# A new order of issue for the whole program of a fused attention and token-mixing kernel

## The chip, the cores and the metric

The kernel runs on one core of one Trainium2 chip. The metric is the device time of one execution in microseconds (us); the time before is 207.22 us, the median of three runs (206.42 to 207.49). The engines are called by their short names: PE (TensorE matmul; PEld is its weight load), DVE (VectorE), ACT (ScalarE), POOL (GpSimd) and SP (SyncE, which here only issues DMAs).

## The reference

Batch 8, heads 8, sequence 576, head dimension 64; 8 x 64 = 512 channels.

```python
kv  = einsum('bhsd,bhse->bhde', k, v)
out = einsum('bhsd,bhde->bhse', q, kv)
rms = sqrt(mean(out*out, -1) + 1e-6)
x   = (out / rms * g_norm)            # heads side by side: (B, 576, 512)
theta = x @ w_theta
zr, zi = x*cos(theta), x*sin(theta)
y   = einsum('ts,bsd->btd', w_tok_r, zr) + einsum('ts,bsd->btd', w_tok_i, zi)
u   = x + y
return u + maximum(u @ w_ch, 0)
```

## The kernel before

The kernel is written as a list of 1189 small tasks, and a separate text, `TURNS`, says in which order they are issued. A task has a name, one or two engines that may run it, a function, and the tasks that it depends on. `play` walks through `TURNS`: a number n issues task n on its first engine, `n*` issues it on its second, and `rN` or `aN` issues N idle matmuls into a PSUM buffer of the `raw` or the `acc` kind. Each engine executes its own tasks strictly in the order in which they were issued, and waits at each for what it needs. So `TURNS` sets the order of every queue: PE, DVE, ACT, the DMAs that SP issues, and POOL with its own DMAs. The numbers shown in time order by the profile are the result of these five queues and their waits.

The 576 rows of a batch are four tiles of 128 (j = 0 to 3) and a tail of 64 (j = 4, marked `e` in names). For each batch b the tasks are, by name:

- **load** k, v (SP; for batch 0 also ACT), their tails (`k0e`, `v0e`), q and the weights (POOL). k and v have two buffers each, so the load of batch b waits for `kv` of batch b - 2. `hold p` is a POOL copy that reads one element of v's tails of batch 0 (L232), so the token weights' loads behind it on POOL are asked for only when those have landed; `hold w` reads the theta weight and holds the load of v of batch 1.
- **kv** (L255, PE): k'v for the heads, in fp32. In batch 0 it comes in pieces: `kvm 0 h` (full tiles of head pair h) and `kvt 0 h` (tails), two pairs to an accumulator. `ko2`/`ko4` (L275 on ACT, L277 on DVE) copy it into the block-diagonal `kbd`, each task as two casts.
- **qt**, `qo`: transpose of q (PE) and the copy `qT` out of PSUM; from batch 3 on q is transposed by a DMA (`qd`, SP).
- **raw** (L312, L321, PE): q times kv. `sq` (L334, ACT) squares, `ss` (L343, DVE) sums, `rt` (L353, POOL) takes the power -1/2, `x` (L375, L384, DVE) multiplies. For batch 0 the root goes by `rs` (L362, ACT) and `rt` (L351, DVE). `raw` has two PSUM buffers from batch 1 on; an `x` frees one.
- **xt**, `xc`: transpose of x (PE) and scaled copy `xT` (L408 on ACT, L410 on DVE); from batch 4 on the transpose is a DMA (`xd`, SP) and `xo` the scaled copy of 1024 columns.
- **th** (L440, L443, PE): theta. `pt` (L456, ACT) rounds the turns to int32, `ar` (L463, DVE) takes the fraction, `ab` (L471 on ACT, L473 on DVE) its absolute value, `si` and `co` (L481, L488, ACT) sine and cosine, `z` (L511, L500, DVE) the products with x.
- **wt** 0 to 8, `wo`: transposes of the token weights and their copies, once, in batch 0.
- **y0**, **y1** (L534, PE): the token mix, for columns 0 to 255 (`y0`) and 256 to 575 (`y1`) of four channel blocks, each in three parts of three matmuls. Part 0 needs z 0 and 1, part 1 needs z 2, part 2 all five. `um` (L539, DVE) makes u.
- **v** (L440, L443; L590 for the two halves of the last batch's tile 1, PE): the channel mix. `ut`, `uo` (or the DMA `ud`) bring u back to rows, `fin` (L576, L596, DVE) makes the output tile, `st` (L613, L617, L604) stores it from SP or POOL.

PSUM is shared by tags: two buffers `tr` for transposes, two `raw`, four `acc` for kv, theta, y and v. A task that opens such a tile waits until an earlier holder's readers are through. All these rules stand in the code as `takes` and `readers`.

Of the kernel before, what the change touches and what calls it, by code (L numbers as in the profile page):

```python
# [29 lines left out]


TURNS = """
3 4 0 1 2 5 6 7 9 8 11 10 13 29 30 41 r1 49 35 14 15 16 17 18 19 22 23 20 21 24 26 207 28 27 42* 57
58* 31 32 36 37 38 33* 34 39* 40* 73 43 74* 50* 44 45 59 75 51 65 25 60 12 61 76 46 66 77 47 62 63
52 r9 48 64 67 53 68 84 82 85 99 54 78 83* 69 70 100 135 139 136 140 79 80 71 55 56 72 92 90 91* 93
86 87* 127 88 101 89* 94 106 120 81 103 102 128* 95 131 137 113 132* 96 138* 104 121 122 105 129 97
114 107 130* 98 108 115 109 143 133 124 123* 134 169 173 141 161 210 211 212 213 110 125 111 144 117
116* 118 142 126 112 119 174 162 216 217* 214 215 170 230 163 223 218 219 231* 165 175 232 171 164
354 203 205 204 206 220 172 176 388 233 221 234 389 166 145 157 167 153 237 224 374 146 154 222 168
225 238* 235 226 236 155 156 227 147 149 244 239 158 375 245 240 251 150 151 187 159 252 241 228 242  # L40
261 253 262 188* 152 148 160 229 381 189 263 243 246 254 382 194 367 255 268 190 368* 256* 177 178*
275 257 182 247 265 264* 266 269 248 249 361 362 363 364 276 270 277 278 267 258* 250 183 279 271*
282 184 259 272 273 283 192 365* 366* 369 383 284 185 260 289 197 199 370 358 209 208 359 360 509
356 357 355 191 529 518 512 513 514 515 371 372 384 193 290 198 274 291 385 195 280 285* 373 281 200
386 292* 293 286 516 294 179 376 387 324 312 404 390 325 377 517 196 540 505 506 507 508 287 180 405
378 316 317 313 402 391 295 288 419 395 314 318 326 392 379 393 380 403 420 396 315 319 327 394 304
397 300 398 399 412 421 400 413 414 519 305 520 401 521 522 408 406 407 320 306 307 296 530 410 531
416 415 422* 423 424 417 411 301 409* 532 533 297 321 302 303 523 308 309 322 323 310 524 525 311
418 534 298 426 427 343 433 548 434 299 428 526 541 542 543 440 441 442 443* 435 544 186 511 527 430
429* 652 653 654 655 658 669 645 646 647 181* 510 425 549* 431 444 656 437 657 344* 545 345 546 554  # L50
563 436 432 555* 346 547* 528 564 445 565 348 584 349 535 536 438 328 556 338 467 468 475 659 585
557 446 439 537 586 339 469 470 558 476 477 455 340 451 452 588 660 329 661 649 785 651 538 650 539
787 662 341 456 670 453 454 560 559* 567 587* 671 672 663 561 457 550 447 552 471 472 458 553 478
673 674 347 680 648 686 473 474 675 333 335 334 336 794 337 805 783 330 676 677 331 577 664 463 589
566* 551 578 568 562 448 449 450 579 464 465 459 665 570 666 678 667 580* 581 571 569 572 466 582
460 461 574 687 668 573* 575 462 679 788 789 790 791 350 681 499 501 351 583 500 682 792 793 502 590
576 688 784 683 684 201* 921 479 699 700 692 693 694 795 489 490 591 685 701 332 503* 342 202 816
781 690 796 797 798 703 611 612 592 494 607 613 614 608 593 594 609 491 806 689* 713 702* 696 807
695* 697 492 808 610 595 619 620 621 481 495 484 596 597 698 799 809 714 715 810 623 782 822 493 930
704 480 482 800 598 622 599 600 811 706 801 802 707 812 705 708 710 709* 691* 615 616 603 604 605  # L60
813 485* 606 803 804 496 617 618 601 486 716* 717 602 786 814 639 817 720 641 487 818 640 819 497
642 924 925 926 927 820 815 821 823 721 722 723 711 718 712 719 928 929* 835 836 483 626 624 625 498
488 824 633 630 634 837 931 828 631 724 932 725 726 747 627 748 755 838* 628 749 936 750 756 727 829
937 938 830 933 743 744 745 757 758 746 735 728 729 730 636 632* 952 917 352* 826 941 919 918 939
934 504* 644* 825 849 751 637 739 740 940 741 947 832 839 831* 833 850 834 759 752 753 851 935 948
949 731 942 736 732 733 950 638* 754 742 842 737 853 840 852* 943 827 843 734 944 777 856 775 854
776 857 920 635 629 1059 951 738 953 760 762 761 945 1053 1054 1055 1056 844 841 946 858 845* 954
846 859* 955 855 778 847 860 956 957 848 1057 861 1058 922 958 1070 862 769 772 763 1060 863 864 770
773 1061 1062 865 959* 866 879 880 881 766 1065 1066 764 882 867 868 964 971 1063 1064 1071 1067 923
771 774* 960 962 1068 767 965 966 869 887 883 884 888 972 973 1069 885 871 1072 1073 765 643 353 895  # L70
1081 768* 1074 779* 974 870 886 967* 975 968 963 976 977 889 890 1075 872 992 1076 875 873 876 961
1077 993 874 994 877 891 892 893 969 996 995* 997 1078 878 978 979 894 970 985 980 986 982 981* 911
1082 913 912* 987 988* 983 914 998 984 908 899 905 1015 1016 989 990 896 780 897 898 1087 900 901
1079 991 999 1000 1017 1001 906 1018 1080 902 1011 1012 1013 903 1002 1083 1088 909 1014 1084 1093
1094 1095 1100 1101 1007 1008 1009 1019 1023 1102 1027 1028 1029 1024 1089 1085 916 1031 904 1086
1096* 1090 1097 1104 907 1091 910 1030 1103* 1025 1003 1004 1005 1020 1021 1010 1026 1006 1107 1022
1105 1098 1092 1106 1099 1108 1114 1115 1109 1121 1110 1047 1034 1033 1049 1048 1050 1116 1038 1041
1111 1122 1123 1112 1113 1124* 1125 1118 1126 1117* 1119 1032 1039 1040 1042 1043* 1156 1035 1036
1144 1157 1148 1149 1145 1152 1153 1127 1120 1146 1150 1154 1158 1151 1147 1155 1159 1037 1044 1136
1132 1045 1180 1178 1137 1138 1139 1179 1181 1133 1128 1183 1185 1173 1140 1141 1134 1184 1186 1129  # L80
1130 1135 1182 1188 1187 1131 1142 1143 1175 1160 1162 1046* 1174* 1176 1161* 1177 915* 1165 1163
1164 1051* 1167 1170 1052* 1166 1168 1171 1169 1172
""".split()


# [845 lines left out]
```

## Time and profile before

| | before |
|---|---|
| median of three runs | 207.22 us (206.42 to 207.49) |
| profiled execution, its own time | 206.56 us |
| span of the profile | 204.6 us |
| PE busy | 188.3 us in 2078 matmuls |
| DVE busy | 172.5 us in 362 instructions |
| ACT busy | 137.6 us in 272 |
| POOL busy | 86.4 us in 92 |
| data moved | 43.14 MB, mean 211 GB/s |

The span runs from the first to the last instruction of the program; the 2 us between it and the execution's own time lie outside. In the profile, "L255" is line 255 of the kernel. A row of a timeline or of the chain that ended last gives the start and the length in us, the engine, the line and the tile names; the chain merges neighbours of one kind (x80 is eighty instructions). In a group row the numbers after the bar are busy time, mean ns of one, and the idle time before them with what ended it. In a window row the values after the stretch are its length and, for PE, PEld, DVE, ACT and POOL, busy time with the count of instructions, then the granted clock, the DMA share and GB/s. A PE that is busy is not a PE at its peak: matmuls overlap, and a wait shorter than a matmul's own length leaves no idle time.

### The profile page before, as it was taken

The page shows a single profiled execution, that of the slowest core. Times are in us where ns is not written, and L with a number is a line of the kernel's source. Part 1 is how long each engine was busy: PE and PEld are TensorE (multiplying, and loading weights), DVE is VectorE, ACT ScalarE, POOL GpSimd, SP SyncE. Part 2 cuts the span into 40 slices and gives each one's busy share as a digit, 9 for nine tenths or more (in the row PEclk, how much of TensorE's full clock was granted, in tenths as well). Part 3 has the DMA queues.
Part 4 walks back from the last instruction along what each step waited for, and adds up shares of the span by engine and source line. Part 5 has one row for each costly group of instructions (what it writes and reads, how often), then busy time and mean ns, then how long its engine had stood idle before and what let it go on. Part 6 is the DMA issues. An engine that isn't in the chain of part 4 may idle for free.

```text
span 204.6 us, 5267 instructions
## 1 busy us (share of the span) xinstructions
PE 188.3 (92%) x2078; PEld 132.8 (65%) x2078; DVE 172.5 (84%) x362; ACT 137.6 (67%) x272; POOL 86.4 (42%) x92
## 2 busy tenths in 40 slices
PE   0299899999999999999999999998989999999992
PEld 0275568885786777676776767665856746755671
DVE  6029896789999999999898999897989999689473
ACT  2006899748799587987896769576945983976101
POOL 8022061263965564874609382283629430101210
PEclk9999999999999999999999999999999999999999
DMA  6999999999999999999999999799988652853154
GB/s 196 271 197 193 294 268 193 275 354 236 254 187 193 277 264 260 310 221 137 199 226 248 237 221 180 170 283 305 287 187 194 150 103 70 189 129 135 35 154 154
DMA packets 74951, 43.14 MB, mean 211 GB/s; under 512 B 44576, under 2 KB 71008, under 8 KB 74928
## 3 DMA queue, kind: packets, MB, share of 16 engines
q1 hardware_dynamic: 58688, 32.12, 66.9%
q0 software_dynamic: 15040, 9.52, 29.9%
q10 hardware_dynamic: 1200, 1.18, 1.7%
q8 instruction: 16, 0.26, 0.5%
q14 instruction: 7, 0.06, 0.1%
HBM read 33.06 MB, written 9.44 MB: 208 GB/s over the span
## 4 chain that ended last, share of the span: by engine, by line
PE 67%; ACT 12%; DVE 8%; DMA 7%; issue 2%; POOL 1%; DVEq 0%; ACTq 0%; POOLq 0%
PE y L534 29%; PE th L440 11%; PE v L440 11%; DMA vt<-in_v_dram 5%; PE kv L255 3%; PE raw L312 3%; DMA uD<-wn 2%; DVE arg L463 2%; ACT kbd L275 2%; ACT sc L488 2%; PE wps L630 2%; ACT sc L481 1%; ACT arg L471 1%; ACT xT L408 1%; PE qps L270 1%
## 5 line engine op out<-in xcount | busy, mean ns | idle before, releaser
L353 POOL TENSOR_TENSOR rt<-ss,mhalf 128x8 f32<-128x8 f32 (+1 forms) x35 | 54.6, 1563 | 65.7 <-DVE ss L343 65.5
L534 PE MATMUL y<-wT,zm 128*128 128x320 f16 (+1 forms) x512 | 76.8, 286 | 0.7 <-DVE ot L576 0.5
L534 PEld LDWEIGHTS <-zm 128*128 128x128 f16 x512 | 48.0, 98 | 15.8 <-issue 1.2
L539 DVE SCALAR_TENSOR_TENSOR wn<-y,gcol,xT 128x320 f16<-128x320 f32 (+1 forms) x64 | 31.0, 511 | 6.7 <-PE y L534 6.3
L440 PE MATMUL th<-wth,xT 128*128 128x512 f16 x128 | 32.1, 380 | 0.9 <-ACT xT L408 0.6
L456 ACT ACTIVATE arg<-th 128x512 int32<-128x512 f32 (+1 forms) x40 | 21.8, 554 | 14.1 <-PE th L440 13.7
L440 PE MATMUL v<-wch,wn 128*128 128x512 f16 x124 | 30.7, 380 | 0.0
L255 PE MATMUL kv<-vt,kt 128*64 128x64 f32 x640 | 21.9, 230 | 9.3 <-DMA vt<-in_v_dram 9.3
L334 ACT ACTIVATE sqb<-raw 128x512 f32<-128x512 f32 x32 | 18.9, 595 | 14.4 <-PE raw L312 14.3
L255 PEld LDWEIGHTS kv<-vt,kt 128*64 128x64 f32 x640 | 20.9, 144 | 10.2 <-issue 9.7
L488 ACT ACTIVATE sc<-arg,quarter 128x512 f16<-128x512 f32 (+1 forms) x40 | 26.6, 675 | 0.3
L463 DVE SCALAR_TENSOR_TENSOR arg<-th,arg 128x512 f32<-128x512 f32 (+1 forms) x40 | 25.0, 632 | 1.9 <-ACT arg L456 1.5
L481 ACT ACTIVATE sc<-arg 128x512 f16<-128x512 f32 (+1 forms) x40 | 22.7, 582 | 3.2 <-DVE arg L463 2.8
L343 DVE TENSOR_REDUCE ss<-sqb 128x8 f32<-128x520 f32 x32 | 22.0, 687 | 2.4 <-ACT sqb L334 2.4
L511 DVE TENSOR_TENSOR zm<-x,sc 128x1024 f16<-128x1024 f16 x32 | 21.8, 686 | 1.8 <-ACT sc L488 1.5
L375 DVE TENSOR_TENSOR x<-raw,rt 128x512 f16<-128x512 f32 x32 | 21.8, 685 | 0.8 <-POOL rt L353 0.5
L440 PEld LDWEIGHTS <-xT 128*128 128x128 f16 x128 | 11.6, 98 | 11.1 <-ACT xT L408 1.0
L440 PEld LDWEIGHTS <-wn 128*128 128x128 f16 x124 | 11.5, 98 | 10.7 <-issue 0.4
L471 ACT ACTIVATE arg<-arg 128x512 f32<-128x512 f32 (+1 forms) x31 | 17.5, 575 | 1.2 <-DVE arg L463 1.1
L534 PE MATMUL y<-wT,zt 128*128 128x320 f16 (+1 forms) x64 | 18.3, 286 | 0.0
L275 ACT CAST kbd<-kv 64x256 f16<-64x256 f32 (+1 forms) x24 | 8.5, 356 | 13.5 <-PE kv L255 13.2
L275 ACT COPY us<-ups 128x512 f16<-128x512 f16 (+1 forms) x17 | 8.5, 498 | 12.6 <-PE ups L270 11.5
(83 smaller groups left out, 229.3 us busy)
## 6 DMA issues: line engine op xcount, KB each, us to landing
vt<-in_v_dram SPq DMA_DIRECT2D x7, 1024.0 KB, 9.8
kt<-in_k_dram SPq DMA_DIRECT2D x7, 1024.0 KB, 7.9
out_dram<-ot SPq DMA_DIRECT2D x24, 256.0 KB, 2.8
qh<-in_q_dram POOLq DMA_DIRECT2D x7, 512.0 KB, 8.6
out_dram<-ot POOLq DMA_DIRECT2D x7, 256.0 KB, 4.0
kt<-in_k_dram SPq DMA_DIRECT2D x2, 512.0 KB, 4.6
vt<-in_v_dram ACTq DMA_DIRECT2D x2, 512.0 KB, 9.0
kt<-in_k_dram SPq DMA_DIRECT2D x8, 128.0 KB, 7.9
```

The source lines that it names most:

```text
L255: nc.tensor.matmul(t[i * D:(i + 1) * D, hp - lo, :], ks, vs, start=(hp == lo and j == 0), stop=(hp == lo + n - 1 and j == NT - 1),)
L343: nc.vector.reduce_sum(out=ss[:], in_=sq_sb.pop((b, j))[:], axis=AXX)
L353: nc.gpsimd.tensor_tensor(out=rt[:], in0=ss[:], in1=mhalf[:, 0:h], op=ALU.pow)
L375: nc.vector.tensor_tensor(out=x_pair[b, p][:, :, a * HC:(a + 1) * HC].rearrange("p t (h e) -> p h t e", e=D), in0=r[:].rearrange("p (h t e ...
L440: nc.tensor.matmul(t[:], piece(kc), w[:, kc, :], start=first, stop=last)
L456: nc.scalar.activation(out=arg[:, 1, :].bitcast(I32), in_=th_ps[b, j][:], func=AFT.Copy, scale=1.0 / TURN)
L463: nc.vector.scalar_tensor_tensor(out=arg[:, 0, :], in0=th_ps.pop((b, j))[:], scalar=1.0 / TURN, in1=arg[:, 1, :].bitcast(I32), op0=ALU.mul ...
L481: nc.scalar.activation(out=sc[:, 0, :], in_=arg_sb[b, j][:, 0, :], func=AFT.Sin, bias=0.0, scale=TURN * SHRINK,)
L488: nc.scalar.activation(out=sc_sb[b, j][:, 1, :], in_=arg_sb.pop((b, j))[:, 1, :], func=AFT.Sin, bias=quarter[:], scale=-TURN * SHRINK,)
L511: nc.vector.tensor_tensor(out=dst, in0=x.unsqueeze(1).broadcast_to((P, 2, w)), in1=sc[:], op=ALU.mult)
L534: nc.tensor.matmul(t[:, 0:hi - lo], s, wT[:, w, lo:hi], start=n == 0, stop=n == len(z) - 1)
L539: nc.vector.scalar_tensor_tensor(out=uTb[b % NUT][:, c, lo:hi], in0=y_ps.pop((b, h, c))[:, 0:hi - lo], scalar=gcol[:, 0:1], in1=xTb[b % NX ...
```

## The change

Only `TURNS` is replaced. Its 1189 tasks are the same, with the same dependencies, functions and transfers. Three things differ: the order of each queue, for some tasks the engine of the two that may run them, and the idle matmuls (`r1`, `r9` become `a3`, `r10`). The new text begins and ends so:

```diff
 TURNS = """
-3 4 0 1 2 5 6 7 9 8 11 10 13 29 30 41 r1 49 35 14 15 16 17 18 19 22 23 20 21 24 26 207 28 27 42* 57
...
+3 0 29 6 7 30 4 1 9 8 5 2 10 11 13 14 15 16 17 18 19 22 24 26 28 27 207 25 a3 49 41 31 32 35 36 37
+38 39 40 33* 50* 42* 34* 57 73 43 51 58* 65 20 21 23 44 12 74* 45 59 75 r10 60 46 76 61 47 77 66 62
...
-1164 1051* 1167 1170 1052* 1166 1168 1171 1169 1172
+1174 1166* 1168 1171 1169 1188* 1172 1187* 1175 1176 1046* 1177
 """.split()
```

Task by task, the places that the prediction speaks of:

```
start, SP    before: k0a k0b k0e v0e g g v1 v1e k1 k1e
             after:  k0a k0b v0e k0e g g v1 k1 k1e v1e
start, PE    before: kvm00 kvm01 qt00 r1 qt02 kvm02 qt01 kvt00 kvt01 kvm03 kvt02 kvt03 qte raw00 raw01 rawe raw02 qt03 r9 raw03 xt01 xt00 th01 wt4 wt6 th00 xte xt02 wt0 ...
             after:  kvm00 kvm01 a3 qt02 qt00 kvt00 kvt01 kvm02 kvm03 kvt02 kvt03 qt01 qte raw00 raw02 qt03 raw01 rawe r10 raw03 xt01 wt6 xt00 th01 xte th00 wt4 xt02 the wt0 ...
start, DVE   before: qo00 qo01 ko2(33) ko2(39) ko2(40) qoe qo02 ss00 g ss01 ...
             after:  ko2(33) qo02 qo00 ko2(34) qo01 g qoe ss00 ss01 ...
start, ACT   before: ko2(34) sq00 sq01 sqe rs00 qo03 ...
             after:  ko2(39) ko2(40) sq00 sq01 rs00 sqe qo03 ...
SP later     before: ... k5 k5e v5 st qd v5e xd40 qd50 st qd51 v6 xd41 v6e ...
             after:  ... k5 k5e v6 v5 v5e xd40 qd50 qd42 st st qd51 st qd60 xd41 v6e ...
end, PE      before: ... y07 v72 ut70 v70 ut71 vh710 vh711
             after:  ... y07 v73 ut70 v70 vh711 ut71 ut72 vh710 v72
end, DVE     before: ... fin72 uo70 fin70 finh710 finh711
             after:  ... fin73 uo70 fin70 uo71 finh710 finh711 fin72
```

(`ko2(33)` and `ko2(34)` are the two copies for head pairs 0 and 1, whose product with q is `raw 0 0` and `raw 0 2`; 39 and 40 are those for pairs 2 and 3.) Both orders do the same PE work before `kv 1 0`.

In batch 2, ACT's cosine of tile 3 (`co 2 3`) stood behind both `ko4 4` copies, `pt 3 1`, `uoe 1 4` and `sq 3 3`, and now stands ahead of the `ko4 4` copies.

Of the tasks that may run on either engine, these many run on each:

| task | ACT before, after | DVE before, after |
|---|---|---|
| xo, xoe (scaled copies after a DMA) | 9, 5 | 3, 7 |
| uoe, uo (copies of u) | 17, 9 | 7, 15 |
| abe, ab (absolute values) | 31, 26 | 9, 14 |
| wo (token weights) | 5, 3 | 4, 6 |
| xc, xce (scaled copies) | 10, 10 | 10, 10 |
| ko2, ko4 (k'v to kbd) | 12, 15 | 6, 3 |
| qo, qoe | 7, 7 | 8, 8 |
| all | 91, 75 | 47, 63 |

Of the stores of full tiles SP issues 17 instead of 24 and POOL 14 instead of 7; of the half tail stores SP issues 9 instead of 7 and POOL 7 instead of 9.

More of the change, by code (lines that the diff above doesn't have):

```diff
@@ L38 @@
[L38 to L52, printed above, removed]
@@ new lines @@
+48 63 64 52 78 53 79 67 68 69 84 85 139 82 54 70 140 99 80 55 71 83* 56 72 90 92 100 91 81 93 101
+102* 103 104 135 86 120 136* 87* 127 88 106 94 89* 128* 131 129 105 132* 130* 113 96 95* 97 121 98
+122 137 133 138* 169 161 114 107 124 134 115 123 143 125 173 141 116* 108 109 126 144 110 111 117
+118 112 142* 210 211 212 213 119 170 162 174 171 216 230 175 354 203 204 205 206 355 356 357 217*
+231* 214 215 218 219 176 172 220 221 165 163 237 166 232 233 164 238* 234 235 223 224* 167 153 154
+155 156 222 168 149 374 150 157 388 375 225 151 158 145 236 389 251 239 187 159 226 227 228 188* 240
@@ new lines @@
+252* 146 147 253 254 367 189 244 241 160 242 152 229 190 243 245 261 262 263 246 368 247 268 255
+256* 248 249 148 381 194 275 269 382 264* 265 266 270 276 182 257 250 258* 267 271 272 273 277 361
+362 363 364 358 191* 209 208 360 509 359 365 274 183* 279 366 177 184 259 282 278 178* 185 260* 283
+284 192 369 383 199 197 289 370 371 512 513 514 515 372 384 193 198* 385 200 280 286 290 195 291
+285* 287 373 516 293 281 292 386 387 179 376 316 180 294 377 378 288 317 324 404 517 325 312 390 405
+295 518 196* 186 529 505 506 395 540 396 379 391 392 393 380 402 419 313 314 326 318 397 403 420 421
@@ new lines @@
+660 555* 669 511 645 646 783 647 648 510 650 538 470 565 661 539 181* 662 785 348 584 457 334 458
+585 567 475 670 476 477 552 556 336 586 349* 663 664 471 671 587* 566 672 673 557 568 478 569 550
+451 452 453 472 473 665 553 551 558 674 447 577 454 474 686 794 680 342 347 805 337 559* 666 560 578
+579 580 561 588 562 589 667 651 463 675 464 459 465 460 461 462 676 677 678 570 571 572 330 448 668
+581 574 582 328 329 449 450 466 573 788 789 790 791 350 499 681 501 575 687 682 792 590 679 331 351
@@ new lines @@
+497 498 353 493 919 814 924 925 926 927 640 721 722 724 719 642 818 643* 723* 725 815 819 726 820
+823* 928 929 710 709* 711 630 627 631 628 821 824 712 786 922 629* 931 828 633 727 942 829 830 634
+728 729 636 932 730 731 743 744 933 934 943 637 944 935 835 836 837 745 746 732 755 756 825* 936 757
+937 838* 945 733 751 849 758 739 946 947 752 753 734 938 839 840 850 851 735 740 741 747 831 832 748
+833 749 736 737 841 939 742 917 952 503 920 826 759 918 632 638* 1059 644 852* 948 853 940 750 754
```

58 lines of the change are left out of this document (25 added, 33 removed).

## The prediction

> **What bounds the kernel now.** I read the page's busy line and chain first, then busy time by stage, then TensorE's timeline wherever a matmul starts later than the one before it allows.
>
> ```profile
> PE 188.3 (92%) x2078; PEld 132.8 (65%) x2078; DVE 172.5 (84%) x362; ACT 137.6 (67%) x272; POOL 86.4 (42%) x92
> ...
> PE 67%; ACT 12%; DVE 8%; DMA 7%; issue 2%; POOL 1%; DVEq 0%; ACTq 0%; POOLq 0%
> ```
>
> ```profile
> 46.00:66.00 20.00, 19.68 (x298) 14.03 (x296) 19.08 (x39) 17.40 (x36) 12.24 (x12) 1.00 1.30 223
> 66.00:90.00 24.00, 23.75 (x278) 16.98 (x277) 23.37 (x50) 19.26 (x42) 14.84 (x15) 1.00 1.13 267
> ...
> 131.00:152.00 21.00, 19.60 (x228) 14.24 (x226) 17.99 (x37) 14.61 (x29) 10.76 (x10) 1.00 1.14 251
> 152.00:175.00 23.00, 23.00 (x177) 14.63 (x176) 22.22 (x45) 14.96 (x28) 9.43 (x9) 1.00 0.58 138
> ```
>
> TensorE (PE) sets the end, with VectorE (DVE) close behind: the third column is PE, the fifth DVE, and between 46 and 90 us DVE works 42.45 of 44 us. A busy share hides short waits, since matmuls overlap. So I price PE's work by its pace:
>
> ```profile
> 44.08 0.33 PE y L534 x3
> ...
> 70.53 0.45 PE xps L270 x8
> ...
> 89.09 0.86 PE v L440 x4
> ...
> 123.52 2.33 PE kv L255 x80
> ...
> 182.87 0.44 PE v L443 x8
> ...
> 185.14 0.41 PE y L534 x3
> ```
>
> Token mix: 96 thirds of 320 columns at 0.41 and 96 of 256 at 0.33, 71.0 us. Theta and channel mix: 63 full tiles at 0.86, two halves at 0.43, 16 tail tiles at 0.44, 62.1. The k'v products: 8 x 2.33, 18.6. The remaining short matmuls (first products and transposes, about 430) at 0.056 each, 24. Sum 175.7 us. PE works from 9.11 to 200.94 (rows below), 191.8 us, so 16.1 us of waits and slow start are all that any order can win. By the same paces 15.1 us of work lie before the row at 32.86 (k'v of batch 1), so 8.6 of the 16.1 fall before it and 7.5 after. Of these 7.5 about half is a tenth of a microsecond here and there. The other half, 3.6 us, I count as nine waits of over 0.15 us, by the starts of matmuls in the timeline; the first and the two largest:
>
> ```profile
> 54.80 1.04 PE L440 MATMUL th<-wth,xT 128*128 128x512 f16 x4 [0.25 <-DVE xT L410]
> ...
> 139.70 0.40 PE L312 MATMUL raw<-kbd,qD 128*128 128x128 f16 x4 [0.89 <-DVE x L375]
> ...
> 151.78 0.70 PE L534 MATMUL y<-wT,zm 128*128 128x320 f16 x4 [0.52 <-DVE ot L576]
> ```
>
> The bracket names what ended the wait: a DVE result each time.
>
> **The change, term by term.** No step, matmul or byte is added. PE's 175.7 us stay, and so do the transfers. What moves is who waits for whom.
>
> *1. Start.* Rows of the time before, first the chain, then the timeline:
>
> ```profile
> 12.63 1.12 PE kv L255 x16
> ...
> 14.28 1.11 PE kv L255 x32
> ...
> 21.53 1.04 PE th L440 x4
> ...
> 32.86 2.48 PE kv L255 x80
> ```
>
> ```profile
> 9.11 1.97 PE L255 MATMUL kv<-vt,kt 128*64 128x64 f32 x32 [9.11 <-DMA vt<-in_v_dram]
> ...
> 11.66 0.43 DVE L277 COPY qT<-qps 128x512 f16<-128x512 f16 x1 [6.73 <-PE qps L270]
> ...
> 13.93 0.17 POOL L232 COPY gate<-vt 1x1 f32<-1x1 f32 x1 [8.74 <-DMA vt<-in_v_dram]
> ...
> 14.71 1.91 DVE L277 CAST kbd<-kv 64x128 f16<-64x128 f32 x6
> ...
> 15.70 1.30 PE L312 MATMUL raw<-kbd,qT 128*128 128x128 f16 x8
> ```
>
> POOL's gate shows v's tails landed by 13.93, and k's tails were asked for just ahead of them. Swapped, the pair is complete when the second has landed, so again near 13.9: I take no gain. Now kvt 0 0 and kvt 0 1 come ahead of kvm 0 2 and kvm 0 3, so the first two kbd copies can start near 14.4, not 14.71. But DVE has queued behind them the query copies qo 0 2 and qo 0 0, which before ran at 11.66 in a pause, and then the second kbd copy: 0.64 (a third of 1.91) + 0.43 + 0.43 and the first half of 0.64, 1.8 us. The first product starts near 16.2 instead of 15.70: +0.5. From there square, sum, root, x, transpose, scaled copy and theta follow in the same kinds, and theta moves from 21.53 to about 22.0. Of the work up to 32.86 the same set is done in both orders; ScalarE (ACT) gets two absolute values and one tail copy more and two other steps fewer. I carry +0.45 through. Bounds 0 (tails earlier) and +1.1: the transposes share two PSUM buffers, and xt 0 0 and wt 0 each follow by one place the copy that must free theirs, so a late copy shows in full.
>
> POOL's hold on the token weights ends with v's tails, so sooner by about one place in SP's queue. The first weight turn comes after theta's start and waited for no DMA before: hidden, nothing.
>
> The pace doubles in these rows: 1.12/16 is 0.070 us per k'v matmul at 12.63, 1.11/32 is 0.035 at 14.28, after PE has been working since 9.11. In the new order three idle fillers and two turns end near 13.2, and PE then stands until the tails land at 13.9. If the doubling is put off by that, 48 matmuls cost 1.7 us more, of which some 0.3 hides behind DVE: a rival below. [...]
>
> *2. Waits after 32.86.* For each of the nine I counted PE's work between the cause and the waiting matmul in both orders, in the paces above. The first (theta 1 3 after its transpose) gets 1.2 us more cover, the largest (raw 6 3, which takes a raw buffer that an x must free) goes from a chain behind two other sums to a cover of 7.6 us, and the third (y1 5 0 0, for a buffer that a finish frees) from 7.3 to 9.2 us. If the accumulator free longest is taken next, hand-overs with under 1.3 us of PE work between the last write and the next taker fall from 18 to 5 after 32.86. Two of the nine stay as they are, theta 2 1 (0.23) and the token mix of batch 2 (0.35 and 0.23, in part). I take 3.0 of 3.6 as removed; bounds 1.5 and 3.6.
>
> *3. New waits.* The first products have two buffers, so each one needs the x of the second before it. Bare chain:
>
> ```profile
> L343 DVE TENSOR_REDUCE ss<-sqb 128x8 f32<-128x520 f32 x32 | 22.0, 687 | 2.4 <-ACT sqb L334 2.4
> L353 POOL TENSOR_TENSOR rt<-ss,mhalf 128x8 f32<-128x8 f32 x28 | 47.2, 1688 | 39.8 <-DVE ss L343 39.6
> ...
> L334 ACT ACTIVATE sqb<-raw 128x512 f32<-128x512 f32 x32 | 18.9, 595 | 14.4 <-PE raw L312 14.3
> ...
> L375 DVE TENSOR_TENSOR x<-raw,rt 128x512 f16<-128x512 f32 x32 | 21.8, 685 | 0.8 <-POOL rt L353 0.5
> ```
>
> That is 3.7 us, 4 with the hand-overs. The shortest covers are 4.4 to 4.7 us (raw 2 2, 1 3, 3 0, 4 2, 3 1); raw 3 0 falls from 5.7 to 4.5 with three DVE steps in the chain: 0.4 taken, 0 to 0.9. From the last theta to the first token mix that needs its z the cover shrinks in batch 2 (7.9 to 5.6 us), 4 (8.5 to 7.3) and 7 (6.4 to 5.8) and grows in 3, 5 and 6. Before, batch 2 just failed to hold:
>
> ```profile
> 87.36 0.45 PE L534 MATMUL y<-wT,zm 128*128 128x320 f16 x2 [0.18 <-DVE zm L511]
> ```
>
> If these chains stayed as long as they are now, the three would cost 2.3 + 1.2 + 0.6 = 4.1. In batch 2 the cosine is moved ahead of the kbd copies that it stood behind, which shortens it by about as much, so I take 0.8; bounds 0 and 4.1. Sum of new waits 1.2, bounds 0 and 5.0.
>
> *4. Engine loads.* ACT gives up 16 steps net and DVE takes them. The dearest are scaled copies:
>
> ```profile
> L408 ACT ACTIVATE xT<-xD,gcol 128x1024 f16<-128x1024 f16 x6 | 6.8, 1139 | 0.0
> ...
> L410 DVE TENSOR_SCALAR xT<-xD,gcol 128x1024 f16<-128x1024 f16 x2 | 1.0, 478 | 0.0
> ```
>
> Over all by such rows ACT falls 8.6 us and DVE gains 4.3, of which +2.2 in batch 1, -1.7 in batch 2, +2.8 in batch 5. Up to each PE step DVE has at most 0.8 us more to do before 90 us, 2 to 3 less between 67 and 94, and up to 3 more after 165, where its share falls. I count no wait for it; rival D does.
>
> *5. SyncE's (SP) queue.* Load v6 now stands ahead of load v5. It waits for the k'v products of batch 4, and v5, xd 4 0, qd 5 0 and three stores wait behind it. PE has 16.4 us of work from there to the k'v of batch 5.
>
> ```profile
> DMA packets 74951, 43.14 MB, mean 211 GB/s; under 512 B 44576, under 2 KB 71008, under 8 KB 74928
> ...
> vt<-in_v_dram SPq DMA_DIRECT2D x7, 1024.0 KB, 9.8
> ```
>
> Two loads with tails, 2.36 MB at the mean rate, take 11.2 us: hidden. At 9.8 us each, one after the other, 19.6: a wait of 3.2. I take nothing, being nearer the rate over the whole run. POOL has seven more full stores; each waits for a finish that DVE does ahead of the next sum, so no root is held: nothing.
>
> *6. End.*
>
> ```profile
> 199.90 1.04 PE L590 MATMUL v<-wch,wn 128*128 128x256 f16 x8
> ...
> 200.72 0.76 DVE L596 SCALAR_TENSOR_TENSOR ot<-v,us 128x256 f32<-128x256 f32 x2
> ```
>
> ```profile
> out_dram<-ot SPq DMA_DIRECT2D x3, 256.0 KB, 2.0
> ...
> out_dram<-ot SPq DMA_DIRECT2D x1, 128.0 KB, 2.1
> ```
>
> PE's last work is now a full v tile with one finish of 0.69 (as long as the x row) and a store of 256 KB. Before, the second half-finish ended at 201.48, 0.54 us after PE; now it is 0.69: +0.15. In the last 10 us a 256 KB store lands in 2.0 us, a 128 KB one in 2.1, so its size adds nothing. Bounds 0 and +0.7, if the last copies and halves hold up the finish queued behind them on DVE.
>
> Sum: +0.45 - 3.0 + 1.2 + 0.15 = -1.2 us. The profiled execution took 206.56 us, 204.6 of it span; it lies 0.66 under the median of three, 207.22, and that within their spread of 1.07. On the profiled time the sum gives 205.4; I put the change on the median: **206.0 us**. About 0.5% (1.0 us) is what a measurement here can tell from no change.
>
> **The rivals.**
> - *A, no new waits:* the z chains are shortened everywhere as in batch 2. For it speaks that so many buffer hand-overs have more room; against it raw 3 0. -3.0 + 0.6 = 204.8.
> - *B, the waits only move:* DVE is as full as before, so what one wait loses another finds: 3.0 new ones, start and end remain. 207.8.
> - *C, the slow pace lasts longer at the start:* +1.4 on the forecast, 207.4. For it speaks the pause from 13.2 to 13.9; against it the fillers.
> - *D, slower: VectorE becomes the bound.* Place: batches 1 and 5. DVE idles 0.92 us from 46 to 66, and batch 1 brings 2.2 us: 1.3 too much. Batch 5 brings 2.8, against 3.0 idle from 131 to 152 but 0.8 from 152 to 175. The point is whether batch 5's extra copies fall after 152. Nothing is then saved: 207.22 + 0.6 + 1.3 = 209.1, and 2.0 more in the worst case. Against it: batch 2's relief follows at once.
> - *E, slower: v5 behind v6,* decided by whether v5 lands over 16.4 us after batch 4's k'v: +3.2 on the forecast, 209.2.
>
> **How the numbers follow.** Forecast 0.40 (0.27 faster, 0.13 within), A 0.18 (faster), B 0.16 (0.12 within, 0.04 slower), C 0.08 (within), D 0.11 and E 0.07 (slower). Faster 0.45, same 0.33, slower 0.22. The likeliest case's own range is 205.0 to 206.9; the whole range, from a little under A to just short of D and E, 204.2 to 208.7.
>
> **What would show it.** Right: theta of batch 0 starts near 22.0 and the first product near 16.2; the waits at 54.80, 139.70 and 151.78 have no counterpart; PE from theta of batch 0 to its last matmul takes 1.5 to 2 us less than the 179.4 us of before. Wrong: k'v of batch 5 waiting for DMA (E), DVE at over 97% over a whole batch with PE waiting for it (D), a per-matmul pace of 0.07 past 14 us (C), or waits for z in batches 2, 4, 7 of over 0.8 us together.

## The result, and the profile after

The new order is slower: 213.88 us, the median of four runs (212.76 to 215.25), against 207.36 for the order before in the same measurement (206.42 to 207.87). The ratio is 1.032, with a 95% interval of 1.024 to 1.041. The forecast was 206.0, with a range up to 208.7. The profiled execution of the new order took 215.25 us, 213.1 of it span; that of before had a span of 204.6, so the two traces lie 8.5 us apart. (A ratio counts only executions within 1.5% of the fastest of their kernel: the four quickest of the ten of e2, which lie between 206.44 and 212.46 us, and all or all but one of every other kernel's.)

From the page of the new order: the busy line, the chain by engine, and the granted clock in 40 slices of the span.

```profile
PE 190.1 (89%) x2081; PEld 133.3 (63%) x2081; DVE 174.9 (82%) x375; ACT 130.9 (61%) x259; POOL 89.5 (42%) x97
...
PEclk9999999999999999999999999975999999999999
...
PE 44%; DMA 18%; DVE 15%; ACT 13%; SPq 4%; issue 3%; DVEq 0%; ACTq 0%
```

Two things are new. In the chain DMA has gone from 7% to 18% and PE from 67% to 44%: the end now hangs on more transfers. And the clock falls to 7 and 5 tenths in the 27th and 28th slice, so one place is near 140 us. Busy time by stage agrees: in one of the stretches that the prediction showed PE is busy for 16.07 us instead of 19.60, at a mean clock of 0.84.

```profile
131.00:152.00 21.00, 16.07 (x105) 10.30 (x105) 12.96 (x26) 7.82 (x14) 6.04 (x5) 0.84 1.04 205
```

Next the two long new transfers in the chain of the new order, and PE's timeline near the second (in brackets: idle time and what ended it):

```profile
42.36 11.48 DMA vt<-in_v_dram
...
130.28 12.75 DMA xD<-x
143.60 1.89 PE th L440 x4
```

```profile
138.09 0.57 PE L534 MATMUL y<-wT,zm 128*128 128x320 f16 x3
143.60 1.89 PE L440 MATMUL th<-wth,xT 128*128 128x512 f16 x4 [4.93 <-DVE xT L410]
...
149.09 1.11 PE L534 MATMUL y<-wT,zm 128*128 128x320 f16 x7
```

The first of the two, a load of v, comes at the end of this section. At the second, PE stands for 5 us ahead of theta of batch 5, tile 3 (`th 5 3`). Its bracket names DVE, but the DVE step is the scaled copy `xo 5 1`, which itself waits for `xd 5 1`, the DMA that transposes x. That DMA took 12.75 us from issue to landing. SP's own rows show what stands around it:

```profile
129.77 0.40 SPq L184 DMA_DIRECT2D vt<-in_v_dram  x1
130.28 4.26 SPq L421 DMA_TRANSPOSE xD<-x  x1
134.58 0.59 SPq L184 DMA_DIRECT2D kt<-in_k_dram  x1
```

The new order asks for `load v7` (1 MB) half a microsecond ahead of `xd 5 1`. Before, `xd 5 1` was asked for first and k's load of the same batch, the first of the two, 2.8 us behind it. The two answers on the tile xD between 118 and 146 us, the new order and then before:

```profile
L421 SPq DMA_TRANSPOSE xD<-x x3: 1242/1296/4257, 119.3 to 142.4; - x3
...
  DMA xD<-x: 5.2, 1
...
DMA to landing us min/median/max: 4.2/5.2/12.8
```

```profile
L421 SPq DMA_TRANSPOSE xD<-x x3: 1227/1282/2600, 116.4 to 130.9; - x3
...
DMA to landing us min/median/max: 3.4/4.7/8.0
```

Three transposing DMAs each. Before, `xd 5 1` is the minimum: asked for at 127.48, landed 3.4 us later. In the new order it is the maximum, and the copy behind it waits 5.2 us. After the stop PE is slow for a while; granted clock (the first of the last three values) by small stretches of the new order:

```profile
143.60:145.00 1.40, 1.40 (x4) 0.57 (x5) 1.40 (x4) 0.00 (x0) 0.00 (x0) 0.50 1.11 351
145.00:147.00 2.00, 2.00 (x12) 1.31 (x11) 1.38 (x3) 1.11 (x2) 1.27 (x1) 0.50 1.26 290
147.00:149.00 2.00, 2.00 (x14) 1.39 (x13) 0.83 (x2) 1.73 (x4) 0.92 (x2) 0.68 1.17 277
149.00:151.00 2.00, 2.00 (x19) 1.58 (x17) 1.57 (x4) 0.51 (x1) 0.00 (x0) 1.00 0.69 212
```

So the 8.5 us between the traces divide as follows. Theta of batch 0 starts at 22.08 instead of 21.53: 0.55. From there to the end of the last matmul PE takes 186.9 us (22.08 to 209.02) instead of 179.4: 7.5. Behind the last matmul 4.1 us remain instead of 3.7: 0.4. The 7.5 hold the stop (5.1 by the starts of matmuls), the slow stretch (2.3, worked out at e4) and 1.4 at k'v of batch 2, which waits for v (53.14 and 0.91 in the row below). Less 0.8, the difference of the other waits over 0.15 us (3.6 before, 2.8 now), and less 0.5 in small change, that is 7.5.

The wait for v has a crossing on SP's queue behind it too: the load of v for batch 2 is asked for at 40.55, behind tails of k whose issue takes SP 3.87 us, and in before at 36.31. Waits of 0.4 to 2.0 us in all for v of batches 2 and 3 show in five of the nine traces with the later part of the new order (the new order, e3, e8, e10, e11), and none over 0.15 us in the four with that of before. No experiment undoes this crossing. The other rows that answer to the prediction's, PE's timeline of the new order:

```profile
13.88 1.62 PE L255 MATMUL kv<-vt,kt 128*64 128x64 f32 x48 [1.36 <-DMA kt<-in_k_dram]
...
16.09 0.88 PE L312 MATMUL raw<-kbd,qT 128*128 128x128 f16 x8
...
22.08 1.03 PE L440 MATMUL th<-wth,xT 128*128 128x512 f16 x4
...
53.14 2.83 PE L255 MATMUL kv<-vt,kt 128*64 128x64 f32 x80 [0.91 <-DMA vt<-in_v_dram]
...
101.83 1.39 PE L255 MATMUL kv<-vt,kt 128*64 128x64 f32 x40
```

### The profile page after: what moved, and what is told of

Read it like the earlier page. It is cut to its first block, busy times and chain, and to the rows that moved or that the text cites. A ratio compares the mean times of both kernels' runs of the same rounds, so it can differ in the third digit from the quotient of the medians.

```text
span 213.1 us, 5259 instructions
## 1 busy us (share of the span) xinstructions
PE 190.1 (89%) x2081; PEld 133.3 (63%) x2081; DVE 174.9 (82%) x375; ACT 130.9 (61%) x259; POOL 89.5 (42%) x97
## 4 chain that ended last, share of the span: by engine, by line
PE 44%; DMA 18%; DVE 15%; ACT 13%; SPq 4%; issue 3%; DVEq 0%; ACTq 0%
PE y L534 21%; PE th L440 8%; DMA xD<-x 8%; PE v L440 6%; DMA vt<-in_v_dram 5%; DMA kt<-in_k_dram 5%; ACT sc L488 3%; DVE ss L343 3%; PE kv L255 2%; ACT arg L456 2%; DVE ot L576 2%; SPq L190 2%; PE raw L312 2%; SPq L184 2%; DVE zt L500 2%
## 5 line engine op out<-in xcount | busy, mean ns | idle before, releaser
L534 PE MATMUL y<-wT,zm 128*128 128x320 f16 (+1 forms) x512 | 78.1, 289 | 0.2 <-DVE zm L511 0.2
L534 PEld LDWEIGHTS <-zm 128*128 128x128 f16 x512 | 48.7, 99 | 16.6 <-issue 1.5
L440 PE MATMUL th<-wth,xT 128*128 128x512 f16 x128 | 33.2, 387 | 5.5 <-DVE xT L410 5.3
L255 PEld LDWEIGHTS kv<-vt,kt 128*64 128x64 f32 x640 | 20.4, 142 | 12.0 <-issue 11.4
L481 ACT ACTIVATE sc<-arg 128x512 f16<-128x512 f32 (+1 forms) x40 | 23.3, 584 | 3.5 <-DVE arg L463 3.4
L440 PEld LDWEIGHTS <-xT 128*128 128x128 f16 x128 | 11.8, 99 | 15.8 <-DVE xT L410 5.8
L275 ACT CAST kbd<-kv 64x256 f16<-64x256 f32 (+1 forms) x30 | 10.5, 350 | 15.3 <-PE kv L255 14.9
L440 PEld LDWEIGHTS <-wn 128*128 128x128 f16 x124 | 11.4, 98 | 11.1 <-issue 0.8
L471 ACT ACTIVATE arg<-arg 128x512 f32<-128x512 f32 (+1 forms) x26 | 15.5, 599 | 0.6 <-DVE arg L463 0.6
L576 DVE SCALAR_TENSOR_TENSOR ot<-v,us 128x512 f32<-128x512 f32 (+1 forms) x23 | 13.4, 591 | 1.3 <-issue 0.5
```

The costliest lines, as they stand in the source:

```text
L255: nc.tensor.matmul(t[i * D:(i + 1) * D, hp - lo, :], ks, vs, start=(hp == lo and j == 0), stop=(hp == lo + n - 1 and j == NT - 1),)
L440: nc.tensor.matmul(t[:], piece(kc), w[:, kc, :], start=first, stop=last)
L481: nc.scalar.activation(out=sc[:, 0, :], in_=arg_sb[b, j][:, 0, :], func=AFT.Sin, bias=0.0, scale=TURN * SHRINK,)
L534: nc.tensor.matmul(t[:, 0:hi - lo], s, wT[:, w, lo:hi], start=n == 0, stop=n == len(z) - 1)
```

## The experiments

The theory (Q): the load of v asked for just ahead of `xd 5 1` on SP's queue delays it, and this one crossing makes the loss, or nearly all of it. The rival (R): the loss belongs to the new order as a whole, other waits would take its place. Two side questions: why PE is slow after the stop, and what the rest of the new order is worth.

| | kernel | time, us | ratio to before (95%) |
|---|---|---|---|
| | the new order | 213.88 | 1.032 (1.024 to 1.041) |
| e1 | new order, `load v7` behind `xd 5 1` | 208.67 | 1.004 (1.000 to 1.008) |
| e2 | before, `load k7` ahead of `xd 5 1` | 210.38 | 1.002 (0.996 to 1.007) |
| e3 | new order, `load v7` issued by ACT | 212.33 | 1.018 (1.009 to 1.027) |
| e4 | new order, idle matmuls in the stop | 212.55 | 1.023 (1.017 to 1.030) |
| e5 | e1 with the start of before | 208.09 | 1.003 (1.000 to 1.005) |
| e6 | before with the start of the new order | 207.51 | 1.004 (1.001 to 1.007) |
| e7 | before, v's tails of batch 0 first | 207.34 | 1.000 (0.997 to 1.003) |
| e8 | e5, one store later | 208.21 | 1.004 (1.002 to 1.007) |
| e9 | new order, half of `load v7` ahead | 209.36 | 1.013 (1.008 to 1.017) |
| e10 | new order, `load k7` ahead too | 213.38 | 1.032 (1.028 to 1.036) |
| e11 | e3 again | 211.74 | 1.024 (1.012 to 1.036) |

Times are medians. The kernel before took 207.48 beside e1 to e4, 207.32 beside e5 to e8 and 206.95 beside e9 to e11.

**e1, the one crossing undone.** Task 919 is `load v7`, 824 is `xd 5 1`; every other queue stays as it is.

```diff
-497 498 353 493 919 814 924 925 926 927 640 721 722 724 719 642 818 643* 723* 725 815 819 726 820
-823* 928 929 710 709* 711 630 627 631 628 821 824 712 786 922 629* 931 828 633 727 942 829 830 634
+497 498 353 493 814 924 925 926 927 640 721 722 724 719 642 818 643* 723* 725 815 819 726 820 823*
+928 929 710 709* 711 630 627 631 628 821 824 919 712 786 922 629* 931 828 633 727 942 829 830 634
```

> The changed order with one task moved: SP issues the load of v of batch 7 right behind the transposing DMA xd 5 1 instead of just ahead of it. Theory 1 (queue): xd 5 1 is late because it stands behind a megabyte on SP's own DMA queue; it lands within 3 to 5 us of its issue instead of 12.75, the 5.2 us wait of theta 5 3 is gone and with it the slow stretch after it (2.3 us): 206 to 208 us, ratio to the kernel before 0.995 to 1.005. Theory 2 (supply): the 16 DMA engines have too much to move around 130 to 143 us, and the transpose lands late wherever it stands; at most 1.5 us are won, 212 us or more. Theory 3 (prediction's rival D): VectorE is the bound and the DMA only the last to be named; also at most 1.5 us.

SP's rows of e1, then its landings of xD between 118 and 146 us, then the granted clock and the chain by engine:

```profile
129.44 1.32 SPq L421 DMA_TRANSPOSE xD<-x  x1
130.87 0.53 SPq L184 DMA_DIRECT2D vt<-in_v_dram  x1
```

```profile
DMA to landing us min/median/max: 4.3/4.5/5.0
```

```profile
PEclk9999999999999999999999999999999999999999
...
PE 57%; DVE 15%; ACT 14%; DMA 7%; issue 3%; POOL 1%; SPq 1%; DVEq 0%; ACTq 0%; POOLq 0%
```

`xd 5 1` lands in 4.5 us, its issue takes 1.32 us instead of 4.26, the clock stays full (1.00 from 122 to 146 us), and DMA's share of the chain is 7% again. Of the 3.2% that the new order loses, this one place makes 2.8 by the ratios, 5.9 us (5.3 by the medians; the stop of 5.1 and the slow stretch of 2.3 are those of the profiled execution, the longest of the four). Q holds against R, and against the theories of supply and of VectorE, under which at most 1.5 us were to be won. What is left, 0.4%, is still not a gain.

**e2, the same crossing put into the order before.**

```diff
-488 824 633 630 634 837 931 828 631 724 932 725 726 747 627 748 755 838* 628 749 936 750 756 727 829
+488 917 824 633 630 634 837 931 828 631 724 932 725 726 747 627 748 755 838* 628 749 936 750 756 727
```

> The order of before with one task moved the other way: SP issues the load of k of batch 7 right ahead of xd 5 1. Theory 1: xd 5 1 lands 8 to 12 us after its issue at about 129, near 138 to 140, and theta 5 3, which started at 136.4, starts 2 to 5 us later, with a slow stretch if the pause is long: 209 to 213 us. Theories 2 and 3: no change beyond 1 us, 206.4 to 208.4.

SP's rows and PE's in the profiled execution of e2 (212.45 us):

```profile
129.19 0.40 SPq L184 DMA_DIRECT2D kt<-in_k_dram  x1
129.70 2.97 SPq L421 DMA_TRANSPOSE xD<-x  x1
```

```profile
141.93 1.24 PE L440 MATMUL th<-wth,xT 128*128 128x512 f16 x4 [4.23 <-ACT xT L408]
```

The same wait arises, with a scaled copy on ACT this time: 11 us to landing. So the crossing alone suffices in that execution. The granted clock hints at how often: it is 0.990 to 0.992 in six of the ten executions, the profiled one (0.992) among them, against 0.995 or more in all ten of e1 (of before's nineteen beside it, two have 0.988 and 0.992). The median of all executions, 210.38, is 2.9 us over before's; in its quickest ones, 206.44, the wait cannot have been there in full, since it alone is 4.4 us. How long a transposing DMA is held behind a load thus changes from execution to execution; in which way the quick ones escape was not seen.

**e3 and e11, the load on another queue.**

```diff
-            k_ += [add(f"load {n}{b}", "SP",
-                       lambda t=t, src=src: heads_in(nc.sync, t, src, b, all8),
+            own, dma = ("ACT", nc.scalar) if (n, b) == ("v", 7) else ("SP", nc.sync)
+            k_ += [add(f"load {n}{b}", own,
+                       lambda t=t, src=src, dma=dma: heads_in(dma, t, src, b, all8),
```

> The changed order, with the load of v of batch 7 issued by ACT on ACT's own DMA queue at the same place of the order; the bytes and their time are the same, only the queue differs. Theory 1 in the strict form (order within one queue): xd 5 1 lands 3 to 5 us after its issue, 206 to 208 us. Theory 2 (supply): both queues share the same 16 engines, so xd 5 1 still lands 8 to 12 us after its issue and the time stays at 212 or more. In between, near 209 to 211, if the engines serve the two queues in turns.

The result lay between: 212.33. Its one profile was of its quickest execution (209.69), so e11 profiles the same kernel again; that profile too is of the quicker of two (210.73 and 212.76).

> The kernel of the third experiment once more (v's load of batch 7 issued by ScalarE), for a second profile: its one profile was of its quickest execution, 209.69 us against a median of 212.33. If its time is lost in the same place as in the new order, the transposing DMA of batch 5 lands 10 us or more after its issue in an execution of 212 us, and TensorE waits there for 3 us or more. Rival, that it is lost elsewhere: landing in about 7 us, and the lost time in waits of ScalarE's steps behind its own issue.

`xd 5 1` landed 7.2 us (e3) and 7.8 us (e11) after its issue, and `th 5 3` did not wait. In these two executions time is lost earlier. The change of engine also changed when the load is asked for: ACT reaches it at 121.4 us in e3 and 122.5 in e11, 7 to 8 us sooner than SP in the new order, and just ahead of three transposing DMAs of u on SP's queue. PE's timeline of e11, its answer on the tile uD between 118 and 134 us, and the same answer of the new order:

```profile
130.71 1.03 PE L440 MATMUL v<-wch,wn 128*128 128x512 f16 x4
133.47 0.49 PE L534 MATMUL y<-wT,zm 128*128 128x256 f16 x3 [1.74 <-DVE ot L576]
```

```profile
  DMA uD<-wn: 2.9, 1
...
  PE y L534: 1.7, 1
...
DMA to landing us min/median/max: 6.5/7.4/8.3
```

```profile
DMA to landing us min/median/max: 4.2/4.2/4.8
```

The three DMAs of u land in 7.4 us instead of 4.2, the finish that needs u waits 2.9 us, and the token mix that needs the finish's buffer 1.7. So in these two executions a load on another queue holds transposing DMAs too. The simple form of Q, that only the order in one queue counts, is not enough. Whether another queue holds them less is not shown, since the load stands at another time ahead of other DMAs. Nor is it known where the other executions lose their time: their granted clock of 0.983 to 0.990, as in the new order (0.984 to 0.991) and against 0.997 in the two profiled ones, points to a long stop of PE that no trace shows (in e4, where idle matmuls fill the stop, it is 0.995 to 1.000).

**e4, PE kept busy in the stop.** 24 idle matmuls, whose result nobody reads, are issued ahead of task 849 (`th 5 3`).

```diff
-937 838* 945 733 751 849 758 739 946 947 752 753 734 938 839 840 850 851 735 740 741 747 831 832 748
+937 838* 945 733 751 a24 849 758 739 946 947 752 753 734 938 839 840 850 851 735 740 741 747 831 832
```

> The changed order with 24 idle matmuls of 512 columns (24 x 0.216 = 5.2 us) issued just ahead of theta 5 3, in the time in which PE stands; they compute nothing that is used. If the slow pace of PE after the wait (2.3 us more for the same matmuls) comes from its having stood, PE goes on at full pace when theta 5 3 starts: 2 us less than the changed order, 211 to 213, granted clock 1.0. If the slow pace has another cause (heat, power, DMA load), the fillers change nothing or add to it: 213 to 215, clock below 0.99. All theories of the wait itself expect the wait to stay.

```profile
137.22 5.34 PE L640 MATMUL idle<-fill,ident 128*128 128x512 f16 x24
142.40 1.03 PE L440 MATMUL th<-wth,xT 128*128 128x512 f16 x4
...
145.62 1.25 PE L534 MATMUL y<-wT,zm 128*128 128x320 f16 x8
```

The stop stays (theta still starts 5.2 us late), but the four theta matmuls take 1.03 us, not 1.89, and the same work from theta to the last row takes 145.62 - 142.40 = 3.22 us, where the new order takes 149.09 - 143.60 = 5.49. The slow stretch thus costs 2.27 us, and it comes from PE's standing, not from the DMAs. The granted clock of 0.50 in the rows above, from 143.60 to 147, is the same thing seen from the other side; e4 has 1.00 from 143 to 147. Two other traces agree: behind the wait of 4.23 us in e2 the clock is 0.58 from 142 to 146, behind that of 1.74 us in e11 it is 1.00 from 134 to 138. From how long a stop on the clock falls was not measured.

**e9 and e10, the dose.** Half of `load v7` ahead of `xd 5 1`, and two loads (v's and k's) ahead of it.

```diff
+            own = lo4 if (n, b) == ("v", 7) else all8
...
+                if own is lo4:
+                    heads_in(nc.sync, t, src, b, hi4)
+                tails_in(nc.sync, t, src, b, all8)
...
-                       lambda t=t, src=src: heads_in(nc.sync, t, src, b, all8),
+                       lambda t=t, src=src, own=own: heads_in(nc.sync, t, src, b, own),
```

```diff
-823* 928 929 710 709* 711 630 627 631 628 821 824 712 786 922 629* 931 828 633 727 942 829 830 634
+823* 928 929 710 709* 711 630 627 631 628 821 917 824 712 786 922 629* 931 828 633 727 942 829 830
```

> The new order with only heads 0 to 3 of v's load of batch 7 (512 KB) ahead of the transposing DMA of x in batch 5; heads 4 to 7 are asked for behind k's load, with the tails. If the transpose waits for what the same queue carries ahead of it, its time from issue to landing lies halfway between that with nothing ahead (4.5 us, e1) and with the whole load ahead (12.75): 8 to 9 us; TensorE waits about 1 us there instead of 5.1, keeps its full pace, and the time falls to 208 to 210 us. Rival, that any load ahead holds it for a fixed time whatever its size: 11 us or more and 212 to 214 us.

> The new order with k's load of batch 7 moved ahead of the transposing DMA as well, so 2 MB stand before it. If the wait goes by the bytes ahead, 8.3 us a megabyte over the 4.5 us without, it lands about 21 us after its issue, TensorE waits 13 us instead of 5.1 at the theta behind it, and the time is 220 to 223 us. Rival, a fixed hold: 12 to 13 us, and the time as it is, 212 to 215 us.

Landings of xD between 118 and 146 us in e9 and in e10 (the maximum is `xd 5 1` in both), and SP's rows of e10:

```profile
DMA to landing us min/median/max: 4.1/5.6/6.6
```

```profile
DMA to landing us min/median/max: 2.7/4.2/11.1
```

```profile
129.34 0.40 SPq L184 DMA_DIRECT2D vt<-in_v_dram  x1
129.79 0.76 SPq L184 DMA_DIRECT2D kt<-in_k_dram  x1
130.65 6.56 SPq L421 DMA_TRANSPOSE xD<-x  x1
```

Neither size went as forecast. With 0, 0.5, 1 and 2 MB ahead the DMA took 4.5 (e1), 6.6, 12.8 (11.0 in e2, 11.8 in e4) and 11.1 us: half a load holds it by less than half, and a second load by nothing more. A price per byte ahead is refuted, and so is a hold that is the same for half a load and a whole one. What all five executions with a load ahead on the same queue have in common is the order of landing, by the trace's landing times of the last load ahead and of `xd 5 1`:

```
               last load ahead landed   xd 5 1 landed
e9  (0.5 MB)          135.53               136.52
e2  (1 MB)            135.97               140.70
e4  (1 MB)            136.48               140.81
after (1 MB)          140.23               143.03
e10 (2 MB)            140.86               141.76
```

`xd 5 1` landed behind the load in all five, by 0.9 to 4.7 us. This goes beyond these five: in each of the thirteen traces all DMAs that SP issues, 103 to 109 of them, landed in the order of their issue (the traces tell their landings by eight semaphores in turn, so neighbours are timed apart). The price could be read from before. Its SP rows show the last transposing DMA of x of batch 5 behind `load k7`, and this DMA, the maximum of before's answer above, took 8.0 us; nothing waited for it:

```profile
130.26 0.53 SPq L184 DMA_DIRECT2D kt<-in_k_dram  x1
130.89 1.23 SPq L421 DMA_TRANSPOSE xD<-x  x1
```

The load's own time to landing (6.1 to 11.1 us in the five executions) thus sets most of the hold. In e9 `xd 5 1` landed 1 us before its scaled copy began, so `th 5 3` did not wait; most of what its profiled execution took beyond before's is a late start (theta of batch 0 at 23.12). Why one load of 1 MB lands in 6.8 us (e2) and another in 10.5 (the new order), and what makes the last 0.9 to 4.7 us, was not settled. More bytes it was not: from 134 to 138 and from 138 to 142 us the new order moved 188 and 128 GB/s, e1 368 and 248.

**e5 and e6, the two halves apart.** e6 takes the new order up to `kv 1 0` and then the order of before, e5 the reverse (with e1's mending).

```diff
-3 4 0 1 2 5 6 7 9 8 11 10 13 29 30 41 r1 49 35 14 15 16 17 18 19 22 23 20 21 24 26 207 28 27 42* 57
...
+3 0 29 6 7 30 4 1 9 8 5 2 10 11 13 14 15 16 17 18 19 22 24 26 28 27 207 25 a3 49 41 31 32 35 36 37
...
```

> The order of e1 (load v7 behind xd 5 1) with the start of before: all tasks up to the first k'v of batch 1 are issued as before, with its r1 and r9. Theory S (the new start costs what the prediction worked out): theta of batch 0 starts near 21.5 to 21.8 instead of 22.2 and the k'v of batch 1 near 32.8, and the time is 0.4 to 0.8 us below e1's, about 207.0 to 207.9. Rival (the start's delay is made up by later waits, as batch 0's z are bound by ScalarE in both): within 0.2 us of e1.

> The mirror image: the changed start up to the first k'v of batch 1, then the order of before. Theory S: first product near 16.1, theta near 22.1 and the whole 0.4 to 0.8 us slower than before, ratio 1.002 to 1.004. Rival: no difference, ratio 0.999 to 1.001.

```profile
22.05 1.03 PE L440 MATMUL th<-wth,xT 128*128 128x512 f16 x4
```

The row is e6's theta of batch 0. The new start alone costs 0.4% (0.1 to 0.7), the new remainder alone 0.3% (0.0 to 0.5), both together (e1) 0.4%. The parts don't add up exactly, but neither holds a gain. e6 came out as theory S has it, though its interval still touches its rival's range; e5 did not: its theta of batch 0 starts at 22.12 and its k'v of batch 1 at 33.38, and by the ratios it lies 0.2 us below e1, which is its rival's forecast. A single profile does not settle the start. Theta of batch 0 begins between 21.53 and 22.29 in the five traces with the start of before, whose earliest is before's own, and between 21.70 and 23.12 in the eight with the new start.

**e7, v's tails first, alone.**

```diff
-3 4 0 1 2 5 6 7 9 8 11 10 13 29 30 41 r1 49 35 14 15 16 17 18 19 22 23 20 21 24 26 207 28 27 42* 57
+3 4 0 1 5 2 6 7 9 8 11 10 13 29 30 41 r1 49 35 14 15 16 17 18 19 22 23 20 21 24 26 207 28 27 42* 57
```

> The order of before with only the two tail loads of batch 0 exchanged: v's ahead of k's on SP. The prediction's term: no gain and no loss, since kvt needs both; the copy that holds the token weights on POOL ends up to 2 us sooner (11.7 to 13.9 instead of 13.93), the first product at 15.7 and the time within 0.3 us of before. Rival: the token loads, asked for sooner, take bandwidth from k's tails and the queries, and the first product moves to 16 or later, +0.3 to +1 us.

POOL's copy ran at 11.57 and the first product started at 15.81. The ratio is 1.000 (0.997 to 1.003): no effect, as the prediction had it.

**e8, the largest wait left.** In e1 the largest wait behind the start is one for a DMA of u. PE's timeline of e1, and what waited for the tile uD between 140 and 160 us:

```profile
151.97 0.27 PE L534 MATMUL y<-wT,zt 128*128 128x256 f16 x1
153.24 1.02 PE L440 MATMUL v<-wch,wn 128*128 128x512 f16 x4 [1.00 <-DVE ot L576]
```

```profile
  DMA uD<-wn: 1.2, 1
...
  PE v L440: 1.0, 1
```

Task 644 is a store (`ste 3 41`) ahead of that DMA on SP's queue; e8 is e5 with the store behind `ud 4 2`.

```diff
-833 749 736 737 841 939 742 917 952 503 920 826 759 918 632 638* 1059 644 852* 948 853 940 750 754
+833 749 736 737 841 939 742 917 952 503 920 826 759 918 632 638* 1059 852* 948 853 940 750 754 762
...
-635* 957 860 847 778 848 760 761 1053 1054 1055 1056 1057 861 1058 855 862 958 962 1070 863 766 772
+957 860 847 778 848 760 761 644 1053 1054 1055 1056 1057 861 1058 855 862 958 962 1070 863 766 772
```

> e5 with one more move: the tail store ste 3 41, which stands on SP between qd 7 0 and the last three transposes of batch 4's u, goes behind them. In e1 the finish of batch 4 waited 1.15 us for these transposes. If SP's queue is what made them late (theory 1 again, a smaller case), they are asked for about 1.3 us sooner, the wait of the channel mix at 151.75 shrinks from 1.2 us to under 0.3, and the kernel takes 0.8 to 1.2 us less than e5: 206.0 to 207.0, below before. If supply is what makes them late, nothing changes against e5.

The wait stayed (1.2 us by the starts of matmuls) and so did the time. The store was not its cause: the last of the three DMAs of u was asked for sooner, yet took 5.4 us to land instead of 3.6 in e5. That is the forecast under which supply makes them late; what slows them is open.

## Why the prediction was wrong, step by step

**The step that failed is 5, SP's queue.** It priced one crossing on that queue (`load v6` ahead of `load v5`), and for that one asked only whether the k'v products would get their data in time. It didn't look at the other loads that were moved, and not at the small transposing DMAs that a moved load gets in front of. "I take nothing" therefore covers a term of +5.1 us for the stop and +2.3 for the half clock (0.50) behind it; e1 takes both away at once, and e2 makes them in the order of before, in its profiled execution. It also covers the 1.4 us for v of batch 2, of which e1's execution happens to have none. "PE's 175.7 us stay, and so do the transfers" was the deeper fault: their bytes stayed, their order did not. Part of it could be read from before: a transposing DMA right behind a 1 MB load took 8.0 us there, the loads of v 9.8 in the median (the row is in step 5). With 9.8 the load asked for at 129.77 lands at 139.6, the scaled copy takes 0.5, and PE, free at 138.5, waits some 1.6 us. The rest of the 5.1, a slower load (10.5) and the 2.8 us behind it, stands in no row of before.

**The priced crossing** came out right: k'v of batch 5 has no bracket at 101.83, so rival E did not happen.

**Steps 2 and 3, the waits, were wrong in their sum.** They are read from e1, where the stop does not cover them. Waits of 0.15 us and more after k'v of batch 1, by the starts of matmuls: before 0.42, 0.19, 0.23, 0.15, 0.23, 0.35, 0.28, 1.05 and 0.68, in all 3.6. All nine are gone, where I had taken off 3.0. In e1 there are nine others: 0.60, 0.32, 0.31, 0.34, 0.49, 0.28, 1.16, 0.24 and 0.20, in all 3.9, where I had put 1.2. Three rows of e1:

```profile
66.16 0.38 PE L270 MATMUL xps<-ident,x 128*128 128x128 f16 x4 [0.44 <-ACT xT L408]
...
109.00 1.02 PE L440 MATMUL v<-wch,wn 128*128 128x512 f16 x4 [0.17 <-DVE kbd L277]
...
129.43 1.04 PE L440 MATMUL th<-wth,xT 128*128 128x512 f16 x4 [0.32 <-DVE xT L410]
```

The removed waits I had counted at their places, the new ones only for two kinds of chain (the first products and z). Of those, one first product shows, with 0.32. By their brackets most of the other new waits stand at scaled copies (0.60 and 0.49), kbd copies (0.34 and 0.28) and the DMA of u (1.16, at e8), which I had not looked at. This is rival B, that the waits only move. PE needs from theta of batch 0 to the end of its last matmul 202.44 - 23.02 = 179.4 us in e1, and 179.4 in before: the gain of 1.8 (3.0 less 1.2) was nil.

**Step 1, the start, was right in its mechanism, and partly by luck in its size.** The tails were complete at 13.88 (13.9 forecast), the first kbd copy ran at 14.37 (14.4), behind it on DVE the query copies and the second kbd copy, the first product started at 16.09 (16.2), theta at 22.08 (22.0). But those 0.55 us compare one execution with one, and by e5 and e6 the new start costs between 0.2 and 0.8 us. Rival C did not occur in the profiled execution: 48 k'v matmuls in 1.62 us are 0.034 each, the doubled pace. In e1's execution, with the same start, the 48 took 2.36:

```profile
14.35 2.36 PE L255 MATMUL kv<-vt,kt 128*64 128x64 f32 x48 [0.18 <-DMA kt<-in_k_dram]
```

That is 0.049 each, so some of them still ran at the slow pace; in e9 it was 2.83. The start of before has the same: the 32 k'v matmuls behind the tails took 1.15 us in before's trace, but 1.98 in e2, e5 and e8 and 1.51 in e7. The slow pace past 14 us thus comes and goes with the execution in both orders, and is no price of the new one.

**Step 4** was right to price nothing: DVE is busy 174.9 us (+2.4, 4.3 forecast), 82% of the span. Rival D, VectorE as the bound, does not show: from 46 to 66 us DVE works 18.21 us (19.08 before), from 66 to 90 us 23.58 (23.37 before), and PE's share there hardly moves (23.39 us, 23.75 before). **Step 6:** the end costs 0.4 instead of 0.15, within its bounds of 0 to 0.7.

Without the one misplaced load the terms as measured are 0.55 for the start, nothing for the waits and 0.4 for the end, some +1 us, and e1 is 0.8 us (0.4%) above before by the ratio, 1.2 by the medians. I had -1.2; the difference is almost all in the waits. With the load it is +6.5 by the medians.

## What to carry to other kernels

When an order of issue changes, list for every queue what each moved transfer now stands ahead of, and price the small urgent DMA behind the large patient one by the large one's landing time, not by bytes (here `xd 5 1` took 11.0 to 12.8 us behind 1 MB and 11.1 behind 2 MB, against 3.4 to 4.5 with no load just ahead). Count the new waits at every kind of hand-over with the care given to those removed: here nine went and nine came, of the same sum. And a stop of PE can cost more than its length: here 2.3 us came on top of 5.1, in a stretch with a granted clock of 0.50 and then 0.68.

## What the runs showed of the hardware

- The DMAs that SP issued landed in the order of their issue, in all thirteen traces (103 to 109 in each).
- Transposing DMAs of x with a load of 1 MB asked for 0.5 to 1.2 us ahead of them on the same queue landed after 7.3 to 12.8 us (ten cases in before, the new order, e2, e4, e6 and e7); `xd 5 1` without it after 3.4 to 4.5. A second megabyte ahead did not lengthen it (11.1).
- The issue itself took longer there in four executions, and SP stood meanwhile: 4.26 us in the new order, 3.44 in e4, 2.97 in e2 and 6.56 in e10, against 1.32 in e1; but 1.28 behind half a load (e9) and 1.23 behind `load k7` in before.
- Another queue did not end the hold: with the load on ACT's queue three transposing DMAs on SP's took 6.5 to 8.3 us, instead of 4.2 to 4.8, and in the new order one asked for at 108.40 on SP, 0.8 us behind a 512 KB load of q on POOL's queue, took 8.2.
